# Zero-weight matmuls beside value matmuls, tile switches in the scheduler, and a lent score bank

## The chip, the cores and the metric

The kernel runs on one core of a Trainium2 chip. The metric is the device time of one execution in microseconds (us). The *granted clock* is the share of TensorE's full clock that the profile records as granted to it; 1 is full speed. Before the change it is 1780 us. All times below are medians; a run over 1.5% above the fastest of its kernel is called slow and left out of ratios.

## The reference

Four blocks in turn, each added to its input, on x of 2048 rows and 512 columns: A, B, A, B. Each has a layer norm ahead.

```python
# A: 32 heads of 16, one shared key and value head
q = (x @ wq).reshape(B, S, H, Dh).transpose(0, 2, 1, 3)
k, v = x @ wk, x @ wv
p = softmax(einsum("bhqd,bkd->bhqk", q, k) * Dh ** -0.5)
o = einsum("bhqk,bkd->bhqd", p, v)            # then heads side by side, @ wo
# B: linear attention, phi(t) = (t + 1 where t > 0, else exp(t)) + 1e-6
kv, z = einsum("bhsd,bhse->bhde", phi(k), v), phi(k).sum(s)
o = (phi(q) @ kv) / (phi(q) @ z + 1e-6)       # then @ wo
```

The weight of the work is A: 32 x 2048 x 2048 exponentials, twice. The kernel cuts them into 4096 *blocks* of 128 keys by 512 queries.

## The kernel before

The program holds its own list scheduler. It simulates the five engines with a duration for every operation, decides in what order each engine issues, and emits that fixed order with semaphores. What the simulation has wrong can therefore turn into waits on the chip: with the cost of a tile switch set to 0 in it, ScalarE waited 38.5 us for score matmuls instead of 4.2 (below).

Matmuls write into `ps`, which the program divides into eight *banks* of 512 columns, numbered 0 to 7. A block takes three steps: a score matmul (32 rows of the array, 128 columns), an exponential, and a value matmul (128 rows, 32 columns). ScalarE takes the exponentials of three blocks in one instruction. VectorE takes some blocks too, with a polynomial in six instructions.

```python
# scores: row group i, 32 rows                                            (L635)
x = e.matmul(bank(b0 + k), lhsT=Kr[r, m, kt*P:(kt+1)*P], rhs=QT[r, ...], start=True, stop=True)
# values: column group c, 32 columns, accumulated in bank 7               (L671)
e.matmul(ps[32*c:32*c+32, 7*512:8*512], lhsT=Vaug[:, kt, :], rhs=src, start=..., stop=...)
# ScalarE: three score banks at once (set 0: banks 0-2, set 1: banks 3-5) (L775)
e.activation(PTA[:, i, 0:m*512], bank(3*s, m*512), ACTF.Exp, scale=SCALE)
# VectorE: its scores are in bank 6                                       (L829)
e.tensor_scalar(out=xT[...], in0=bank(6), ...)
...
# set 1 filled with 2 blocks only, where bank 5 may be lent:
if s == 1 and SHARE and (not banks.free[5] or (not banks.free[6] and self.waiting())):
    w = 2
```

Bank 6 is shared: every projection, transpose and output tile needs it too. `SHARE` is False before, so bank 5 is never lent to them.

When the simulated TensorE has nothing to do and its recent activity is under a target, the scheduler adds a full-array matmul with zero weights into bank 7. It changes no result and is there to keep TensorE's clock up (with 461 of them instead of 1234 the clock was 0.937 to 0.951 instead of 0.997 to 1.000, below):

```python
FILL, FILLW, FILLN = 0.6, 1.7, 512
def streaming(now):          # activity over the last FILLW us
    ...
        st = {"pv": 0.071, "sA": 0.2, "dummy": 0.2}.get(o.name, 0.85 * o.dur[PE])
def idle(now):
    if not sc.order[PE] or streaming(now) > FILL * FILLW:
        return
    ...                                                                   # (L897)
    o = add(PE, 0.03 + FILLN*0.41e-3, lambda e: e.matmul(bank(7, FILLN), lhsT=zer[:],
            rhs=maskx[:].bitcast(BF16)[:, 0:FILLN], start=not owned, stop=True, ...), name="dummy")
```

The softmax here doesn't subtract the row's maximum and nothing guards it: scores larger than these inputs give would overflow.

## Time and profile before

| | before |
|---|---|
| time | 1780.14 us (1778.29 to 1781.13, 3 runs) |
| ScalarE / VectorE / TensorE busy | 97% / 87% / 95% |
| granted clock of TensorE | 0.998 |
| blocks on ScalarE / VectorE | 3618 / 478 |
| full zero matmuls | 1234 |

The first lines are from the page of the kernel before: busy us, share and instruction count of each engine, and the granted clock in tenths over 40 slices of the span.

```profile
PE 1683.0 (95%) x11642; PEld 533.4 (30%) x11642; DVE 1554.0 (87%) x2767; ACT 1728.1 (97%) x1452; POOL 31.3 (2%) x46
...
PEclk9999999999999999999999999999999999999999
```

The groups of the same page: line, engine, operation, output and inputs, shapes, count, then busy us and mean ns of one, then idle time of the engine before them and what ended it.

```profile
L775 ACT ACTIVATE PTA<-ps_all 128x1536 bf16<-128x1536 f32 x1207 | 1644.0, 1569 | 7.7 <-PE ps_all L635 6.3
L635 PE MATMUL ps_all<-QT,Kr 32*128 32x512 bf16 x4096 | 611.3, 385 | 39.8 <-ACT PTA L775 14.8
L671 PE MATMUL ps_all<-PTA,Vaug 128*32 128x512 bf16 x3618 | 520.1, 390 | 8.2 <-DVE Eo L683 7.8
L897 PE MATMUL ps_all<-maskx,zer 128*128 128x512 bf16 x1234 | 401.0, 386 | 0.0
L829 DVE TENSOR_SCALAR xT<-ps_all 128x512 int32<-128x512 f32 x478 | 327.4, 685 | 80.8 <-PE ps_all L635 78.9
```

ScalarE's exponentials take 1644 us and wait 7.7 us in all. Time can be won by giving ScalarE fewer blocks. VectorE could take more: it stands still 80.8 us ahead of L829, mostly for score matmuls.

Two stretches of 50 us of the kernel before, from the table of stretches: busy us and instructions of each engine, then the clock.

```profile
core 0: us, PE busy (x) PEld busy (x) DVE busy (x) ACT busy (x) POOL busy (x), PEclk, DMA share, GB/s
200.00:250.00 50.00, 47.55 (x324) 13.79 (x324) 47.52 (x83) 49.82 (x39) 0.99 (x1) 1.00 0.00 1
250.00:300.00 50.00, 47.39 (x340) 15.09 (x338) 36.23 (x61) 50.00 (x42) 0.00 (x0) 1.00 0.00 1
```

In the second stretch block B's projections for a part of the rows use bank 6, and VectorE falls from 47.5 to 36.2 us. That is what lending a second bank aims at.

Last, a piece of the timeline of the kernel before: start, duration, engine, line.

```profile
311.12 0.39 PE L635 MATMUL ps_all<-QT,Kr 32*128 32x512 bf16 x1
311.44 0.39 PE L671 MATMUL ps_all<-PTA,Vaug 128*32 128x512 bf16 x2
311.76 0.60 PE L897 MATMUL ps_all<-maskx,zer 128*128 128x512 bf16 x2
312.30 0.39 PE L635 MATMUL ps_all<-QT,Kr 32*128 32x512 bf16 x3
```

Two value matmuls in different column groups take as long as one (0.39 us for the two at 311.44, and 0.39 for a single one at 310.76). Two full matmuls take 0.60 where one takes 0.39, so a pass costs 0.21 us. From one tile shape to another the starts are 0.32 us apart: the change of shape costs about 0.11 us more than a pass.

### The profile page before, as it was taken

How to read it: one execution, taken by the hardware profiler on the slowest of the kernel's cores; microseconds unless marked ns; L12 is line 12 of the kernel's file. 1: busy time of each engine (PE TensorE's matmuls, PEld its weight loads, DVE VectorE, ACT ScalarE, POOL GpSimd, SP SyncE). 2: the span in 40 equal slices, each digit the busy share in tenths (PEclk: the TensorE clock that was granted, in tenths of full speed). 3: DMA queues.
4: the chain of work that ended last, by engine and by line, in shares of the span. 5: the costliest groups of instructions: out<-in, count | busy, mean ns of one | idle time of the engine just before them, and what ended most of it. 6: DMA issues, size and time to landing. Idle time of an engine off the chain costs nothing.

```text
span 1777.9 us, 27691 instructions
## 1 busy us (share of the span) xinstructions
PE 1683.0 (95%) x11642; PEld 533.4 (30%) x11642; DVE 1554.0 (87%) x2767; ACT 1728.1 (97%) x1452; POOL 31.3 (2%) x46
## 2 busy tenths in 40 slices
PE   7999999999999999999899999999999999999998
PEld 4222222222232222233442222322222322222334
DVE  7999997999887998878789999879998879978775
ACT  7999999999999999999699999999999999999996
POOL 0000000000000000000000000000000000000000
PEclk9999999999999999999999999999999999999999
DMA  3000000000000000000000000000000000000001
GB/s 120 1 1 1 1 1 1 1 1 1 1 1 1 1 1 1 1 1 1 1 1 1 1 1 1 1 1 1 1 1 1 1 1 1 1 1 1 1 1 48
DMA packets 7724, 9.14 MB, mean 5 GB/s; under 512 B 1456, under 2 KB 7088, under 8 KB 7600
## 3 DMA queue, kind: packets, MB, share of 16 engines
q1 hardware_dynamic: 7600, 7.37, 1.3%
q8 instruction: 91, 1.49, 0.3%
q14 instruction: 33, 0.27, 0.1%
HBM read 5.28 MB, written 2.10 MB: 4 GB/s over the span
## 4 chain that ended last, share of the span: by engine, by line
ACT 62%; PE 19%; DVE 17%; issue 1%; DMA 0%; POOL 0%; SPq 0%
ACT PTA L775 60%; PE ps_all L635 6%; PE ps_all L671 5%; PE ps_all L897 3%; DVE xT L829 3%; DVE PTD L851 3%; PE ps_all L496 2%; ACT e_buf L939 1%; DVE xs L847 1%; DVE xu L846 1%; DVE xs L850 1%; DVE stats L461 1%; PE ps_all L1060 1%; DVE xs L848 1%; DVE xu L849 1%
## 5 line engine op out<-in xcount | busy, mean ns | idle before, releaser
L775 ACT ACTIVATE PTA<-ps_all 128x1536 bf16<-128x1536 f32 x1207 | 1644.0, 1569 | 7.7 <-PE ps_all L635 6.3
L635 PE MATMUL ps_all<-QT,Kr 32*128 32x512 bf16 x4096 | 611.3, 385 | 39.8 <-ACT PTA L775 14.8
L671 PE MATMUL ps_all<-PTA,Vaug 128*32 128x512 bf16 x3618 | 520.1, 390 | 8.2 <-DVE Eo L683 7.8
L897 PE MATMUL ps_all<-maskx,zer 128*128 128x512 bf16 x1234 | 401.0, 386 | 0.0
L829 DVE TENSOR_SCALAR xT<-ps_all 128x512 int32<-128x512 f32 x478 | 327.4, 685 | 80.8 <-PE ps_all L635 78.9
L635 PEld LDWEIGHTS ps_all<-QT,Kr 32*128 32x128 bf16 x4096 | 147.2, 91 | 486.3 <-ACT PTA L775 188.1
L851 DVE SCALAR_TENSOR_TENSOR PTD<-xT,xs 128x1024 uint16<-128x1024 int32 x239 | 290.3, 1215 | 1.8
L671 PEld LDWEIGHTS ps_all<-PTA,Vaug 128*32 128x32 bf16 x3618 | 126.2, 93 | 319.0 <-issue 299.9
L846 DVE TENSOR_SCALAR xu<-xT 128x1024 f16<-128x1024 uint16 x239 | 164.3, 687 | 3.7
L847 DVE TENSOR_TENSOR xs<-xu 128x1024 f16<-128x1024 f16 x239 | 163.5, 684 | 2.9
L850 DVE TENSOR_TENSOR xs<-xs,xu 128x1024 f16<-128x1024 f16 x239 | 163.0, 682 | 2.4
L897 PEld LDWEIGHTS ps_all<-maskx,zer 128*128 128x128 bf16 x1234 | 93.9, 97 | 196.5 <-issue 179.4
L671 PE MATMUL ps_all<-PTD,Vaug 128*32 128x512 bf16 x478 | 128.8, 388 | 18.2 <-DVE Eo L683 11.4
L848 DVE TENSOR_SCALAR xs<-xs 128x1024 f16<-128x1024 f16 x239 | 98.9, 414 | 1.7
L849 DVE TENSOR_SCALAR xu<-xu 128x1024 f16<-128x1024 f16 x239 | 99.2, 415 | 0.0
L496 PE MATMUL ps_all<-wqkv_sb,xnT 128*128 128x512 bf16 x256 | 68.7, 382 | 1.5 <-DVE xT L829 0.9
L940 DVE TENSOR_SCALAR e_buf<-e_buf 128x512 f32<-128x512 f32 x64 | 27.1, 423 | 45.4 <-ACT e_buf L939 45.2
L469 POOL TENSOR_TENSOR rstd<-veps,mhalf 128x1 f32<-128x1 f32 x30 | 27.8, 925 | 1668.5 <-DVE veps L467 1668.5
L939 ACT ACTIVATE e_buf<-ps_all 128x512 f32<-128x512 f32 x64 | 46.0, 719 | 4.8 <-PE ps_all L496 3.1
L671 PEld LDWEIGHTS ps_all<-PTD,Vaug 128*32 128x32 bf16 x478 | 28.2, 93 | 65.2 <-DVE PTD L851 30.7
L461 DVE BATCH_NORM_STATS2 stats<-x_sb 128x6 f32<-128x512 bf16 x64 | 43.2, 680 | 3.8 <-DMA x_sb<-in_A_x_dram 2.9
L683 DVE COPY Eo<-ps_all 128x512 f32<-128x512 f32 x62 | 42.4, 684 | 4.3 <-PE ps_all L671 3.7
(87 smaller groups left out, 825.9 us busy)
## 6 DMA issues: line engine op xcount, KB each, us to landing
out_dram<-x_sb SPq DMA_DIRECT2D x16, 128.0 KB, 1.7
x_sb<-in_A_x_dram SPq DMA_DIRECT2D x3, 512.0 KB, 6.9
wqkv_sb<-in_B_wqkv_dram SPq DMA_DIRECT2D x1, 1536.0 KB, 11.3
x_sb<-in_A_x_dram SPq DMA_DIRECT2D x2, 256.0 KB, 3.1
wq_sb<-in_A_wq_dram SPq DMA_DIRECT2D x1, 512.0 KB, 5.1
wo_sb<-in_A_wo_dram SPq DMA_DIRECT2D x1, 512.0 KB, 8.3
wo_sb<-in_B_wo_dram SPq DMA_DIRECT2D x1, 512.0 KB, 10.9
wk_sb<-in_A_wk_dram SPq DMA_DIRECT2D x1, 16.0 KB, 2.5
```

Of the source, the lines that this page charges most:

```text
L496: i = e.matmul(bank(h.idx, n), lhsT=l, rhs=r, start=(c + k == 0), stop=(c + k == len(mms) - 1))
L635: x = e.matmul(bank(b0 + k), lhsT=Kr[r, m, kt * P:(kt + 1) * P], rhs=QT[r, self.units[u][0] % 2, gs, q0:q0 + n], start=True, stop=True)
L671: return e.matmul(ps[32 * c:32 * c + 32, 7 * 512:8 * 512], lhsT=Vaug[:, kt, :], rhs=src, start=opened[0], stop=opened[1], skip_group_check ...
L775: oe = add(AC, tac(m * 512), lambda e: e.activation(PTA[:, hp.idx, 0:m * 512], bank(3 * s, m * 512), ACTF.Exp, scale=SCALE), deps=[o] + pr ...
L829: o = add(DV, tdv(512), lambda e: e.tensor_scalar(out=xT[:, hx.idx, i * 512:(i + 1) * 512], in0=bank(6), scalar1=SCALE * LOG2E * 65536.0, ...
L846: o = add(DV, tdv(w, 0.52), lambda e: e.tensor_scalar(out=u_, in0=lo, scalar1=1.0 / 65536, scalar2=-0.5, op0=ALU.mult, op1=ALU.add), deps= ...
L847: o1 = add(DV, tdv(w, 0.52), lambda e: e.tensor_tensor(out=s_, in0=u_, in1=u_, op=ALU.mult), deps=[o] + c["prev"], name="xsq", **kw)
L848: o2 = add(DV, tdv(w, 0.26), lambda e: e.tensor_scalar(out=s_, in0=s_, scalar1=XK, scalar2=-XW, op0=ALU.mult, op1=ALU.add), deps=[o1], nam ...
L849: o3 = add(DV, tdv(w, 0.26), lambda e: e.tensor_scalar(out=u_, in0=u_, scalar1=1.0, scalar2=XL, op0=ALU.mult, op1=ALU.add), deps=[o1], nam ...
L850: o4 = add(DV, tdv(w, 0.52), lambda e: e.tensor_tensor(out=s_, in0=s_, in1=u_, op=ALU.mult), deps=[o2, o3], name="xc", **kw)
L851: o5 = add(DV, tdv(w), lambda e: e.scalar_tensor_tensor(out=PTD[:, hp.idx, 0:w].bitcast(U16), in0=xT[:, k, 0:w], scalar=2.0 ** -9, in1=s_, ...
L897: o = add(PE, 0.03 + FILLN * 0.41e-3, lambda e: e.matmul(bank(7, FILLN), lhsT=zer[:], rhs=maskx[:].bitcast(BF16)[:, 0:FILLN], start=not ow ...
```

## The change

Its intent has three parts. (1) *Riders*: zero-weight matmuls of 32 columns are started beside a value matmul, in column groups that it leaves unused, so that activity costs no time; full ones stay for when activity is low. (2) The scheduler models TensorE better: passes of 0.217 us, column groups side by side, and 0.1 us for a change of tile shape. (3) `SHARE = True`: bank 5 is lent. The diff, cut to its core (many changed durations left out):

```diff
+SWITCH, PASS = 0.1, 0.217
+    def pe_need(self, o):
+        k, g = o.pk
+        if k != self.pk:
+            return self.pend_t + SWITCH
+        return self.pend_t if k == "F" else max([self.pgrp.get(x, 0.0) for x in g])
...
-    FILL, FILLW, FILLN = 0.6, 1.7, 512
-    SHARE = False
+    AWIN, ATGT, AFREE = 2.4, 0.44, 0.6
+    SHARE = True
...
-    def streaming(now):
+    def activity(now):
...
+                k = o.pk[0]
+                w = RG / P * len(o.pk[1]) if k == "S" else 0.4 if k == "P" else 0.95
+                tot += w * (min(end, now) - max(o.t0, now - AWIN))
+        return tot / AWIN
...
+        if owned and last.pk[0] == "P" and now - last.t0 < 0.03 and a < AFREE:
+            for c in range(4):
+                if sc.pgrp.get(c, 0.0) <= now:
+                    o = add(PE, PASS, lambda e, c=c: e.matmul(ps[32*c:32*c+32, 7*512:8*512], lhsT=zer[:, 0:32],
+                                      rhs=maskx[:].bitcast(BF16)[:, 0:512], start=False, stop=True, ...), name="dp")
...
+        if a > ATGT:
             return
...     # then one full zero matmul, as before
```

`activity` counts a rider like a value matmul, at 0.4 of its time: both are of kind "P".

More of the change, by code (lines that the diff above doesn't have):

```diff
@@ L17 @@
 FLEX = 0.0
+SWITCH, PASS = 0.1, 0.217
 class Op:
     __slots__ = ("engs", "fn", "dur", "prio", "deps", "nleft", "succ", "rt", "guard", "acq", "uses", "rel", "cb",
-                 "eng", "t0", "vis", "idx", "gidx", "waits", "marked", "val", "vc", "dma", "done", "name")
+                 "eng", "t0", "vis", "idx", "pk", "gidx", "waits", "marked", "val", "vc", "dma", "done", "name")
 class Holder:
@@ L64, in __init__ @@
         self.idle = lambda now: None
+        self.pk, self.pgrp, self.pend_t = "F", {}, 0.0
     def add(self, engs, dur, fn, reads=(), writes=(), prio=5.0, guard=None, acq=(), uses=(), rel=(), cb=None, deps=(),
-            dma=False, name=""):
+            dma=False, name="", pk=("F", ())):
         o = Op()
+        o.pk = pk
         o.engs = engs if isinstance(engs, tuple) else (engs,)
@@ L128, in _try @@
             cand = sorted(ready, key=lambda r: (r[0] + (FLEX if len(r[2].engs) > 1 and self.act_ok(r[2]) else 0.0), r[1]))
+        limit = None
         for i, (p, s, o) in enumerate(cand):
@@ L131, in _try @@
                 continue
+            if e == PE:
+                need = self.pe_need(o)
+                if need > self.now + 1e-9:
+                    if limit is None or need < limit:
+                        limit = need
+                        self.at(need, None)
+                    continue
+                if limit is not None and self.now + o.dur[PE] > limit + 0.03:
+                    continue
             if e == AC and len(o.engs) > 1 and not self.act_ok(o):
@@ L167, in _start @@
         end = self.now + o.dur[e]
+        if e == PE:
+            if o.pk[0] != self.pk:
+                self.pk, self.pgrp = o.pk[0], {}
+            for x in o.pk[1]:
+                self.pgrp[x] = end
+            self.pend_t = max(self.pend_t, end)
         o.vis = end + (3.0 if o.dma else LAT[e])
-        self.tfree[e] = end
-        self.at(end, None)
+        self.tfree[e] = end if e != PE or o.pk[0] == "F" else self.now + 0.004
+        self.at(self.tfree[e], None)
         self.at(o.vis, None)
@@ L480, in tr @@
             return i
-        o = add(PE, 0.45, tr, reads=["ident"], deps=[o], uses=[hx], acq=[hb], rel=[hx], prio=prio, name="tr")
+        o = add(PE, 0.22, tr, reads=["ident"], deps=[o], uses=[hx], acq=[hb], rel=[hx], prio=prio, name="tr")
         def cp(e):
@@ L498, in proj @@
             kw = dict(acq=[h]) if c == 0 else dict(uses=[h], deps=[o])
-            o = add(PE, len(part) * (0.03 + n * 0.36e-3), f, reads=reads, prio=prio, name=name, **kw)
+            o = add(PE, len(part) * (0.006 + n * 0.42e-3), f, reads=reads, prio=prio, name=name, **kw)
         return o
@@ L527, in f @@
             return k
-        o = add(PE, 0.16 * n, f, reads=["wv"] + [("xnT", t) for t in range(t0, t0 + n)], acq=[h], prio=prio, name="vp")
+        o = add(PE, 0.1 * n, f, reads=["wv"] + [("xnT", t) for t in range(t0, t0 + n)], acq=[h], prio=prio, name="vp")
         def ev(e):
@@ L558, in q_tile @@
             kw = dict(acq=[h]) if c == 0 else dict(uses=[h], deps=[o])
-            o = add(PE, 0.55, f, reads=["wq", ("xnT", t)], prio=prio, name="qt", **kw)
+            o = add(PE, 0.445, f, reads=["wq", ("xnT", t)], prio=prio, name="qt", **kw)
         def ev(e):
@@ L667, in cb @@
                     self.norm(u, o)
+            c = (j % NRG) * (4 // NRG) + j // NRG
             def f(e):
-                c = (j % NRG) * (4 // NRG) + j // NRG
                 return e.matmul(ps[32 * c:32 * c + 32, 7 * 512:8 * 512], lhsT=Vaug[:, kt, :], rhs=src, start=opened[0], stop=opened[1],
                                 skip_group_check=True)
-            o = add(PE, 0.1, f, reads=[("V", kt)], deps=[dep], uses=[hold], rel=[hold] if last else [], prio=2.0 + 1e-4 * u, guard=guard, cb=cb, name="pv")
+            o = add(PE, PASS, f, pk=("P", (c,)), reads=[("V", kt)], deps=[dep], uses=[hold], rel=[hold] if last else [], prio=2.0 + 1e-4 * u, guard=guard, cb=cb, name="pv")
             return o
@@ L693, in tr @@
                 return i
-            o = add(PE, 1.0, tr, reads=["identf"], deps=[oe], acq=[ht, hos] if par == 0 else [ht], uses=[he], rel=[he], prio=1.2, name="trA")
+            o = add(PE, 0.48, tr, reads=["identf"], deps=[oe], acq=[ht, hos] if par == 0 else [ht], uses=[he], rel=[he], prio=1.2, name="trA")
             o = add(DV, 0.168, lambda e: e.reciprocal(rden[:, hr.idx, :].unsqueeze(2), bank(ht.idx).rearrange("p (a c) -> p a c", c=32)[:, :, DH:DH + 1]),
@@ L769, in f @@
                 return self.smm(e, got, 3 * s)
-            o = add(PE, 0.2 + 0.014 * m if RG == 32 else 0.05 + 0.14 * m, f, reads=self.keys(got), deps=prev, uses=[h], prio=0.0, name="sA")
+            o = add(PE, PASS * (-(-m * RG // P)), f, reads=self.keys(got), deps=prev, uses=[h], prio=0.0, name="sA",
+                    pk=("S", tuple(dict.fromkeys(self.parts(q)[0] for q in got))))
             hp = Holder(p_pta)
@@ L827, in dstep @@
             banks.hist[6] = []
-            o = add(PE, 0.22, lambda e: self.smm(e, [p], 6), reads=self.keys([p]), deps=prev, uses=[h], prio=1.5, name="sD")
+            o = add(PE, PASS, lambda e: self.smm(e, [p], 6), reads=self.keys([p]), deps=prev, uses=[h], prio=1.5, name="sD", pk=("S", (self.parts(p)[0],)))
             o = add(DV, tdv(512), lambda e: e.tensor_scalar(out=xT[:, hx.idx, i * 512:(i + 1) * 512], in0=bank(6), scalar1=SCALE * LOG2E * 65536.0,
@@ L874, in bass_interleave_layers__grouped_kv_mqa__linear_attn_block__prompt_kernel @@
     sc.step = ctl.step
-    def streaming(now):
+    def activity(now):
         tot = 0.0
         for o in reversed(sc.order[PE]):
-            if o.t0 + 1.5 < now - FILLW:
+            if o.t0 + 1.5 < now - AWIN:
                 break
-            st = {"pv": 0.071, "sA": 0.2 if RG == 32 else 0.4, "dummy": 0.2}.get(o.name, 0.85 * o.dur[PE])
             end = o.t0 + o.dur[PE]
-            if end > now - FILLW:
-                tot += st * min(1.0, (end - (now - FILLW)) / o.dur[PE])
-        return tot
+            if end > now - AWIN:
+                k = o.pk[0]
+                w = RG / P * len(o.pk[1]) if k == "S" else 0.4 if k == "P" else 0.95
+                tot += w * (min(end, now) - max(o.t0, now - AWIN))
+        return tot / AWIN
     def idle(now):
-        if not sc.order[PE] or streaming(now) > FILL * FILLW:
+        if not sc.order[PE] or any(not d.done or d.vis > now for d in (sc.lastw["mask"], sc.lastw["zer"])):
             return
@@ L892, in idle @@
         owned = u >= 0 and 0 < sum(ctl.count[u]) < 64
-        if not owned and not banks.free[7]:
+        if not owned and (not banks.free[7] or any(d.vis > now for d in banks.hist[7])):
             return
-        if owned and now < sc.tfree[AC] < now + 0.1:
-            return
-        o = add(PE, 0.03 + FILLN * 0.41e-3, lambda e: e.matmul(bank(7, FILLN), lhsT=zer[:], rhs=maskx[:].bitcast(BF16)[:, 0:FILLN], start=not owned, stop=True, skip_group_check=True),
+        last = sc.order[PE][-1]
+        a = activity(now)
+        if owned and last.pk[0] == "P" and now - last.t0 < 0.03 and a < AFREE:
+            for c in range(4):
+                if sc.pgrp.get(c, 0.0) <= now:
+                    o = add(PE, PASS, lambda e, c=c: e.matmul(ps[32 * c:32 * c + 32, 7 * 512:8 * 512], lhsT=zer[:, 0:32], rhs=maskx[:].bitcast(BF16)[:, 0:512],
+                                                              start=False, stop=True, skip_group_check=True),
+                            reads=["mask", "zer"], prio=9.0, pk=("P", (c,)), name="dp")
+                    banks.hist[7].append(o)
+                    sc._start(PE, o)
+                    return
+        if a > ATGT:
+            return
+        need = sc.pend_t + (0.0 if sc.pk == "F" else SWITCH)
+        if need > now + 1e-9:
+            sc.at(need, None)
+            return
+        if any(not o.done and not o.acq and (o.guard is None or o.guard()) for (_, _, o) in sc.ready[PE]):
+            return
+        if owned and now < sc.tfree[AC] + LAT[AC] < now + PASS + SWITCH:
+            return
+        o = add(PE, PASS, lambda e: e.matmul(bank(7), lhsT=zer[:], rhs=maskx[:].bitcast(BF16)[:, 0:512], start=not owned, stop=True, skip_group_check=True),
                 reads=["mask", "zer"], deps=[] if owned else list(banks.hist[7]), prio=9.0, name="dummy")
         banks.hist[7].append(o)
-        sc._try(PE)
+        sc._start(PE, o)
     sc.idle = idle
@@ L916, in tr @@
             return i
-        o = add(PE, 0.45, tr, reads=["ident", ("Osb", g % 2, 0), ("Osb", g % 2, 1)], acq=[h], uses=[hos], rel=[hos], writes=keys, prio=pr, name="otr")
+        o = add(PE, 0.22, tr, reads=["ident", ("Osb", g % 2, 0), ("Osb", g % 2, 1)], acq=[h], uses=[hos], rel=[hos], writes=keys, prio=pr, name="otr")
         def cp(e):
@@ L985, in pq_tile @@
             kw = dict(acq=[h]) if g == 0 else dict(uses=[h], deps=[o])
-            o = add(PE, 0.27, f, reads=["wqkv", ("xnT", t)], prio=pr, name="pq", **kw)
+            o = add(PE, 0.224, f, reads=["wqkv", ("xnT", t)], prio=pr, name="pq", **kw)
         phi(h, o, pqT[:, :, ts], [("pq", g, t) for g in range(NG)], 2.4, tiled=True)
@@ L1006, in kv_block @@
                 rd = [t] if i > 0 else tl
-                o = add(PE, 0.22, f, reads=[(k, tt) for k in ("pk", "vB") for tt in rd], prio=3.4, name="kv", **kw)
+                o = add(PE, 0.172, f, reads=[(k, tt) for k in ("pk", "vB") for tt in rd], prio=3.4, name="kv", **kw)
             dst = kvacc if b == 0 else kvtmp
@@ L1050, in den @@
             return i
-        o = add(PE, 0.3, den, reads=[("zb", g) for g in range(NG)] + [("pq", g, t) for g in range(NG)], acq=[win, hd], prio=pr - 0.4, name="den")
+        o = add(PE, 0.223, den, reads=[("zb", g) for g in range(NG)] + [("pq", g, t) for g in range(NG)], acq=[win, hd], prio=pr - 0.4, name="den")
         o = add(AC, tac(512), lambda e: e.activation(e_buf[:, he.idx, :], bank(hd.idx), ACTF.Ln, bias=1e-6), deps=[o], uses=[hd], acq=[he], rel=[hd], prio=0.4 + 0.01 * t, name="ln")
```

## The prediction

> **What bounds the kernel now.** By the page's busy table ScalarE works 1728.1 of 1777.9 us (97%), TensorE is marked 95%, VectorE 87%. The chain that ended last is 60% the ScalarE exponential (PTA, L775). In the table of stretches ScalarE is busy 1635 of 1643 us between 30:850 and 912:1735; nearly all its 50 us of idleness lie in the start, the layer change (850:912) and the tail. Steady time is won only by giving ScalarE less to do.
>
> The other exponential path is VectorE: 478 of 4096 score blocks. By the groups one block costs it 0.685 + half of (687+684+414+415+682+1215) ns = 2.73 us; one ScalarE block costs 1644/3618 = 0.454 us. VectorE is idle 189 us in the two steady stretches. The waits name the reason: L829 for score matmuls 78.9 us, e_buf for ScalarE 45.2, v_tok and x_sb for projections 36. L829 has one PSUM bank, shared with every projection, transpose and phi tile. In stretches without such work VectorE is busy about 49 of 50 us (20 blocks), with it 36 to 44 (10 to 12 blocks).
>
> **What the change does.**
> 1. SHARE lends bank 5 of the second ScalarE set to that other work; VectorE's scores keep bank 6. Cost: ScalarE fills of 2 blocks instead of 3. Chained 1536-column instructions take 1.343 us; at 0.83 ns a column about 0.064 us is fixed, so a two-block fill loses about 0.021 us. I estimate 200 to 450 such fills: 4 to 10 us.
> 2. Full-array zero matmuls (1234, 401 us marked) mostly give way to 32-column ones that start beside a value matmul. I estimate 1000 to 2500 riders and 200 to 600 full ones. [...]such tiles run concurrently; this trace agrees (three value matmuls in 0.40 us, one in 0.39), so riders should cost almost nothing.
> 3. The scheduler models the tile switch. [...]the trace shows weight-load gaps of 0.23 us ("issue") between score and value groups. This should cut badly placed waits of VectorE, not ScalarE's work.
>
> **Sum.** If half of VectorE's 189 us is recovered, that is about 34 more blocks: -34 x 0.454 = -15 us. Two-block fills: +6. Earlier score matmuls and projections at start and layer change: -5. Result: about 1763 us, -0.9%. All of VectorE's idleness would be worth 31 us before the fills' cost, so over 2% is unlikely.
>
> Predicted 1763 us, 8 in 10 between 1742 and 1784. Faster by over 2%: 0.13; within 2%: 0.80; slower by over 2%: 0.07.
>
> **What would show it.** Step 1: L829's count rises from 478 to about 512, its wait for score matmuls falls below 45 us, VectorE reaches 90 to 92%; L775 splits into 1536- and 1024-column forms. Step 2: far fewer 128-wide zero matmuls, many 32-wide ones, value-matmul groups as short as now. Step 3: ScalarE stays at 97%; its wait for score matmuls stays under 15 us. PEclk stays at 9.
>
> **What would make it wrong.** The target of TensorE's activity falls from 0.6 to 0.44, on another scale; if riders count for less than assumed, the granted clock (0.998 now) dips and both paths wait. If two-block fills are many hundreds, or the shorter instruction exposes the other set's refill, the gain is eaten. If start and layer change (each 10 to 15 us of ScalarE idleness) improve much, it could pass 2%.

"This trace agrees" in step 2 is the measurement that the forecast for riders rests on: three value matmuls take 0.40 us at 301.62 in before and one takes 0.39 at 300.65. The 0.83 ns a column of step 1 had no measurement beside it. The trace of after shows it: starts of chained exponentials are 1.331 us apart after three blocks and 0.905 after two, by the medians, so 0.426 us for 512 columns, with 0.05 us left as fixed where the prediction had 0.064.

## The result, and the profile after

| | before | after |
|---|---|---|
| time | 1780.64 us (4 runs) | 1873.89 us (1870.09 to 1882.06, 4 runs) |
| granted clock | 0.998 | 0.831 in the profiled run, 0.823 to 0.840 |
| ScalarE / VectorE busy | 97% / 87% | 93% / 87% |
| blocks on ScalarE / VectorE | 3618 / 478 | 3574 / 522 |
| full zero matmuls / riders | 1234 / 0 | 218 / 1376 |

The ratio is 1.0532, with a 95% interval of 1.0495 to 1.0569: 5.3% slower. Ratios here are the mean time of one kernel's fast runs over that of the other's of the same rounds, so not quite the ratio of the medians quoted. The counts of zero matmuls, blocks and two-block fills are read from the orders that the programs emit; the trace of after has its riders whole, but its group of full zero matmuls shows 128 of the 218.

The page of the kernel after, the same lines as before:

```profile
PE 1655.4 (88%) x11844; PEld 490.4 (26%) x12002; DVE 1636.2 (87%) x2944; ACT 1733.1 (93%) x1528; POOL 29.2 (2%) x46
...
PEclk9678878859896788988797787988769886888988
```

Its groups:

```profile
L803 ACT ACTIVATE PTA<-ps_all 128x1536 bf16<-128x1536 f32 (+1 forms) x1284 | 1646.8, 1430 | 91.0 <-PE ps_all L661 86.1
L661 PE MATMUL ps_all<-QT,Kr 32*128 32x512 bf16 x4096 | 738.0, 450 | 154.0 <-ACT PTA L803 111.6
L698 PE MATMUL ps_all<-PTA,Vaug 128*32 128x512 bf16 x3574 | 598.8, 457 | 5.3 <-DVE Eo L710 4.6
L929 PE MATMUL ps_all<-maskx,zer 128*32 128x512 bf16 x1376 | 439.8, 469 | 0.0
L857 DVE TENSOR_SCALAR xT<-ps_all 128x512 int32<-128x512 f32 x522 | 358.3, 686 | 93.2 <-PE ps_all L661 91.1
```

VectorE took more blocks, as meant. But the exponentials now wait 91 us, 86 of them for score matmuls, where they waited 7.7. A score matmul went from 385 to 450 ns on average, a value matmul from 390 to 457. Nothing was added to these matmuls; the clock under them went down (0.998 to 0.831). The table of stretches, cut along one stretch of low clock, the next of full clock and the next of low, shows the machine in both conditions:

```profile
core 0: us, PE busy (x) PEld busy (x) DVE busy (x) ACT busy (x) POOL busy (x), PEclk, DMA share, GB/s
52.60:86.30 33.70, 32.76 (x181) 6.96 (x182) 28.40 (x50) 28.39 (x21) 0.00 (x0) 0.50 0.00 0
86.90:120.40 33.50, 28.32 (x231) 8.71 (x230) 32.45 (x59) 33.43 (x29) 0.99 (x1) 1.00 0.00 1
120.90:144.30 23.40, 22.65 (x136) 4.89 (x136) 21.20 (x37) 21.05 (x16) 0.00 (x0) 0.50 0.00 1
```

At clock 1.00 ScalarE is busy 33.43 of 33.50 us. At 0.50 TensorE itself is full (32.76 of 33.70), ScalarE gets 28.39 and runs 21 instructions where it ran 29. There is no third value in this trace: its clock records have only 1.0 and 0.5. The low stretches last from 3.413 to 44.373 us, 635 us in 41 of them, and each is a whole multiple, 1 to 13 times, of the shortest. (A 42nd, of 0.39 us, lies at the end of the records, after the span.) The same records of before show two stretches of 3.413 us. In the longest low stretch of after TensorE was marked busy 42.75 of 44.30 us (376.50:420.80), and the clock stayed at half all the while.

The clock records and ScalarE's instructions together tell where ScalarE stood still. I added up, for each profiled run, the gaps between ScalarE's instructions that fall into low and into full clock (from the first clock record on, which comes 11.3 us after the start in before and 11.2 in after):

```
kernel                  low clock us   ScalarE idle in low clock   in full clock
before                          6.8                  1.6                38.4
after                         635                   99.3                31.0
```

The span grew by 1873.3 - 1777.9 = 95 us; ScalarE's idleness in the tally grew by 130.3 - 40.0 = 90 us and its work by 5. All of the growth falls into low clock (1.6 to 99.3 us); in full clock idleness did not grow (38.4 to 31.0 us, in a full-clock time that is some 530 us shorter, so this is no gain of the new order). So the loss lies in the low-clock stretches. What brought them about is a matter for experiments.

A piece of the timeline of after, in low clock:

```profile
68.33 0.61 PE L698 MATMUL ps_all<-PTA,Vaug 128*32 128x512 bf16 x3
68.33 0.61 PE L929 MATMUL ps_all<-maskx,zer 128*32 128x512 bf16 x1
68.73 0.63 PE L698 MATMUL ps_all<-PTD,Vaug 128*32 128x512 bf16 x1
68.73 0.63 PE L929 MATMUL ps_all<-maskx,zer 128*32 128x512 bf16 x1
```

Riders do run side by side with value matmuls and cost no pass of their own: three value matmuls and a rider, started together at 68.33, take 0.61 us. In full clock, at 101.72, they take 0.40 us, as three value matmuls without a rider do in before (at 301.62).

### The profile page after: what moved, and what is told of

It is laid out like the page before. It is cut to its first block, busy times and chain, and to the rows that moved or that the text cites. A ratio compares the mean times of both kernels' runs of the same rounds, so it can differ in the third digit from the quotient of the medians.

```text
span 1873.3 us, 28558 instructions
## 1 busy us (share of the span) xinstructions
PE 1655.4 (88%) x11844; PEld 490.4 (26%) x12002; DVE 1636.2 (87%) x2944; ACT 1733.1 (93%) x1528; POOL 29.2 (2%) x46
## 4 chain that ended last, share of the span: by engine, by line
ACT 53%; PE 34%; DVE 12%; issue 1%; DMA 0%; SPq 0%; POOL 0%; ACTq 0%
ACT PTA L803 50%; PE ps_all L661 14%; PE ps_all L698 12%; DVE xT L857 2%; PE ps_all L719 2%; PE ps_all L522 2%; DVE PTD L879 2%; ACT e_buf L987 1%; PE ps_all L945 1%; PE ps_all L1108 1%; DVE xs L875 1%; DVE xs L878 1%; DVE xu L874 1%; DVE stats L487 1%; PE ps_all L929 1%
## 5 line engine op out<-in xcount | busy, mean ns | idle before, releaser
L803 ACT ACTIVATE PTA<-ps_all 128x1536 bf16<-128x1536 f32 (+1 forms) x1284 | 1646.8, 1430 | 91.0 <-PE ps_all L661 86.1
L661 PE MATMUL ps_all<-QT,Kr 32*128 32x512 bf16 x4096 | 738.0, 450 | 154.0 <-ACT PTA L803 111.6
L698 PE MATMUL ps_all<-PTA,Vaug 128*32 128x512 bf16 x3574 | 598.8, 457 | 5.3 <-DVE Eo L710 4.6
L929 PE MATMUL ps_all<-maskx,zer 128*32 128x512 bf16 x1376 | 439.8, 469 | 0.0
L857 DVE TENSOR_SCALAR xT<-ps_all 128x512 int32<-128x512 f32 x522 | 358.3, 686 | 93.2 <-PE ps_all L661 91.1
L879 DVE SCALAR_TENSOR_TENSOR PTD<-xT,xs 128x1024 uint16<-128x1024 int32 x261 | 316.8, 1216 | 0.8
L698 PE MATMUL ps_all<-PTD,Vaug 128*32 128x512 bf16 x522 | 169.0, 470 | 13.7 <-DVE PTD L879 10.9
L929 PEld LDWEIGHTS ps_all<-maskx,zer 128*32 128x32 bf16 x1376 | 89.8, 97 | 1.1 <-issue 0.8
L719 PE MATMUL ps_all<-identf,Eo 128*128 128x128 f32 x256 | 58.3, 369 | 3.9 <-DVE Eo L710 1.7
L945 PE MATMUL ps_all<-maskx,zer 128*128 128x512 bf16 x128 | 54.9, 472 | 1.6 <-issue 0.9
```

The costliest lines, as they stand in the source:

```text
L661: x = e.matmul(bank(b0 + k), lhsT=Kr[r, m, kt * P:(kt + 1) * P], rhs=QT[r, self.units[u][0] % 2, gs, q0:q0 + n], start=True, stop=True)
L698: return e.matmul(ps[32 * c:32 * c + 32, 7 * 512:8 * 512], lhsT=Vaug[:, kt, :], rhs=src, start=opened[0], stop=opened[1], skip_group_check ...
L803: oe = add(AC, tac(m * 512), lambda e: e.activation(PTA[:, hp.idx, 0:m * 512], bank(3 * s, m * 512), ACTF.Exp, scale=SCALE), deps=[o] + pr ...
L857: o = add(DV, tdv(512), lambda e: e.tensor_scalar(out=xT[:, hx.idx, i * 512:(i + 1) * 512], in0=bank(6), scalar1=SCALE * LOG2E * 65536.0, ...
L879: o5 = add(DV, tdv(w), lambda e: e.scalar_tensor_tensor(out=PTD[:, hp.idx, 0:w].bitcast(U16), in0=xT[:, k, 0:w], scalar=2.0 ** -9, in1=s_, ...
L929: o = add(PE, PASS, lambda e, c=c: e.matmul(ps[32 * c:32 * c + 32, 7 * 512:8 * 512], lhsT=zer[:, 0:32], rhs=maskx[:].bitcast(BF16)[:, 0:51 ...
```

## The experiments

The theory: the clock falls because 1016 full zero matmuls were taken out and what replaced them, the riders, does not hold it up. Rivals: riders do as much as the scheduler assumes and only the target is too low; the lent bank or the new order exposes ScalarE, and the clock is a symptom; it is their zero data that makes riders worthless. Fifteen kernels were run, each beside the kernel before on the same chip. "Fills of two" are ScalarE instructions of two blocks.

### The bank lent alone

```diff
 # before.py
-    SHARE = False
+    SHARE = True
```

> The kernel before with the bank lent (SHARE = True) and nothing else of the change; its schedule has 1070 full zero matmuls, 542 VectorE score blocks and 362 two-block ScalarE fills. My theory (the loss comes only from the granted clock, the lent bank is sound): clock stays above 0.98, ScalarE's wait for score matmuls below 20 us, time 1780 - 64 x 0.454 + 362 x 0.021 = about 1759 us (1750 to 1772). Rival (the lent bank and the short fills themselves expose ScalarE and VectorE to waits): 1785 us or more at a clock above 0.98.

Measured: 1801.30 us, ratio 1.0118 (1.0092 to 1.0144), clock 0.992 to 0.999. Here my theory was wrong and the rival right: in the old order lending loses 1.2% at a high clock. The wait of ScalarE for score matmuls in this kernel (us in total, times, longest):

```profile
ACT PTA L775 <- PE ps_all L635: 32.2, 91, 1.0
```

Before, this wait was 6.3 us in 23 waits. By my tally ScalarE is idle 67.1 us in full clock. In a list of its gaps of over 0.1 us in full clock ahead of L775 (29.9 us in all), 22.5 us stand right behind an instruction of two blocks: it ends about 0.4 us sooner than one of three, and the other set is not refilled yet. (Starts of chained exponentials are 1.331 us apart after three blocks and 0.904 after two, by the medians; that is 0.83 ns a column and 0.05 us fixed, so by itself a two-block fill loses about 0.02 us, as the prediction said.) A two-block fill thus costs more than its own overhead (22.5 us of gaps behind 362 of them are 0.06 us each), unless the order knows better.

### The riders not emitted, all else in the same order

```diff
 # after.py
+    gone = {id(o) for o in sc.all if o.name == "dp"}
+    sc.all = [o for o in sc.all if id(o) not in gone]
+    sc.order[PE] = [o for o in sc.order[PE] if id(o) not in gone]
...  # renumber, and take them out of the dependencies
     sc.finalize()
```

> The kernel after with exactly its order on every engine, but the 1376 riders are not emitted. My theory (a rider beside a value matmul adds no activity[...]): clock as after, 0.83 within 0.02, time 1874 us within 12. Rival (riders count as the scheduler assumes, 0.4 of their time, and only the target is too low): the activity falls by a further 0.07 of each stretch, so clock below 0.75 and time above 1920 us.

Measured: 1882.21 us, ratio 1.0565 (1.0521 to 1.0609), clock 0.813 to 0.833. Its clock row:

```profile
PEclk9778879668997569988797787879679875798888
```

Taking away 1376 riders moved the clock by some 0.01 to 0.02 and the time by less than the intervals tell apart (after: 1.0495 to 1.0569). The rival's clock below 0.75 did not come. These 1376 riders hold the clock up little or not at all.

### Both targets raised

```diff
 # after.py
-    AWIN, ATGT, AFREE = 2.4, 0.44, 0.6
+    AWIN, ATGT, AFREE = 2.4, 0.6, 0.75
```

> The kernel after with both activity targets raised (0.44 to 0.60, riders 0.60 to 0.75): 696 full zero matmuls, 1779 riders, 518 VectorE blocks, 271 two-block fills. My theory (too few full zero matmuls let the clock fall to half in stretches, and this is the whole loss): clock above 0.95, ScalarE's wait for score matmuls below 25 us, time 1755 to 1785 us. Rival (new order, tile-switch model and lent bank lose the time, the clock is a symptom of the waits): clock may rise but the time stays above 1820 us.

Measured: 1766.53 us (1761.55 to 1777.56), ratio 0.9940 (0.9904 to 0.9976), clock 0.979 to 0.995. With 696 full zero matmuls instead of 218 the loss is gone and a gain of 0.6% stands. Its clock row and ScalarE's wait for score matmuls:

```profile
PEclk9999999999999999999999999999999999999999
...
ACT PTA L803 <- PE ps_all L661: 4.2, 9, 0.6
```

The lent bank, the new scheduler and the riders are all still there, so none of them was the loss. Its four runs also show the price of the clock: 1761.55 us at 0.995, 1764.32 at 0.993, 1768.75 at 0.987, 1777.56 at 0.979.

### Full zero matmuls only

```diff
 # after.py
-    AWIN, ATGT, AFREE = 2.4, 0.44, 0.6
+    AWIN, ATGT, AFREE = 2.4, 0.56, -1
```

> The kernel after without any rider and the full target at 0.56: 926 full zero matmuls, 515 VectorE blocks, 294 two-block fills. My theory: clock above 0.98, time 1780 - 37 x 0.454 + 294 x 0.021 = about 1769 us (1758 to 1778), so faster than before, without a single rider. Rival (riders are needed to hold the clock once the full ones are cut by a quarter): clock below 0.95, time above 1790 us.

Measured: 1772.12 us, ratio 0.9970 (0.9949 to 0.9992), clock 0.983 to 0.991. As expected: no rider is needed.

### The zero matmuls of before made narrow

```diff
 # before.py, L897
-    e.matmul(bank(7, FILLN), lhsT=zer[:], rhs=...
+    e.matmul(ps[0:32, 7 * 512:7 * 512 + FILLN], lhsT=zer[:, 0:32], rhs=...
```

> The kernel before with its 1234 full zero matmuls made 32 columns wide (128 rows, alone in the array, same places in the order). My theory ([...]a rider fails because a value matmul streams at the same time anyway): clock above 0.98, time 1780 to 1800 us. Rival A (a 32-column zero matmul is seen as a quarter of the array, or not at all, wherever it stands): clock below 0.90, time above 1830 us.

Measured: 1772.51 us, ratio 0.9968 (0.9948 to 0.9989), clock 0.989 to 0.998. From its page:

```profile
PEclk9999999999999999999999999999999999999999
...
L897 PE MATMUL ps_all<-maskx,zer 128*32 128x512 bf16 x1234 | 398.2, 384 | 0.0
```

The very instruction that is worthless as a rider, 32 columns with zero weights, holds the clock nearly as well as a full one when it streams alone (0.989 to 0.998, against 0.997 to 1.000 of before in the same round). So neither its width nor its zeros can be what fails it in the change; what is left of the differences is that another matmul of the same shape streams at the same time. "Nearly" has to be said: low clock takes 37.5 us of its trace, against 6.8 before. The time came out below the expected 1780. A narrow zero matmul has the tile shape of the value matmuls, and the idle time of weight loads ahead of L897 falls from 196.5 to 74.1 us; that this is what saved the time is not shown, for ScalarE's wait for score matmuls did not fall (8.9 us, 6.3 before).

### The target of before lowered

```diff
 # before.py
-    FILL, FILLW, FILLN = 0.6, 1.7, 512
+    FILL, FILLW, FILLN = 0.42, 1.7, 512
```

> The kernel before with its target lowered (0.60 to 0.42): 461 full zero matmuls instead of 1234, 484 VectorE blocks; no lent bank, no riders, no tile-switch model. My theory: the cut of full zero matmuls alone brings the clock down, to 0.80 to 0.95, time 1800 to 1870 us. Rival (the clock falls only with the new order or the lent bank): clock above 0.985, time below 1785 us.

Measured: 1811.46 us, ratio 1.0201 (1.0151 to 1.0250), clock 0.937 to 0.951. From its page:

```profile
PEclk9999989957899989999999989997999999899999
```

With 461 full zero matmuls and nothing else of the change, the old order loses its clock as well.

### Riders with non-zero weights

```diff
 # after.py, L929
-    lhsT=zer[:, 0:32], rhs=...
+    lhsT=ident[:, 0:32], rhs=...
```

> The kernel after with riders that hold the identity in place of zeros, so that they carry non-zero weights (the result is wrong on purpose). My theory (concurrency, not zero data, makes a rider worthless): clock as after, 0.83 within 0.03, time 1860 to 1890 us. Rival B[...]: clock above 0.90, time below 1830 us.

Measured: 1875.96 us, ratio 1.0545 (1.0524 to 1.0566), clock 0.829 and 0.831. No change. Rival B, that zero weights are the cause, had expected a clock above 0.90, so they are not. This test is weaker than the one with narrow zero matmuls, because the identity has one non-zero weight in a column and the moving operand is mostly zero. (The small error it adds stayed within the tolerance of the comparison.)

### The new scheduler alone

```diff
 # after.py
-    AWIN, ATGT, AFREE = 2.4, 0.44, 0.6
-    SHARE = True
+    AWIN, ATGT, AFREE = 2.4, 0.55, -1
+    SHARE = False
```

> The kernel after without riders and without the lent bank, target 0.55: 967 full zero matmuls, 461 VectorE blocks, practically no two-block fills; so the tile-switch model alone, at a high clock. My theory (the model alone wins nothing, because ScalarE was not waiting before; it only makes lending safe): clock above 0.98, time 1780 + 17 x 0.454 = about 1788 us (1780 to 1796). Rival (the model by itself is the gain seen in the kernels with target raised): below 1773 us.

Measured: 1784.57 us, ratio 1.0034 (1.0019 to 1.0049), clock 0.989 to 0.991. As the theory had it: without a lent bank the model of the tile switch wins nothing.

### A corrected count of activity

```diff
 # after.py, in activity(); and AWIN, ATGT, AFREE = 1.7, 0.48, -1
-                w = RG / P * len(o.pk[1]) if k == "S" else 0.4 if k == "P" else 0.95
-                tot += w * (min(end, now) - max(o.t0, now - AWIN))
+                lo, hi = max(o.t0, now - AWIN), min(end, now)
+                if k == "P":                      # value matmuls side by side count once
+                    tot += max(0.0, min(hi, seen) - lo)
+                    seen = min(seen, lo)
+                else:
+                    tot += (RG / P * len(o.pk[1]) if k == "S" else 0.95) * (hi - lo)
```

> The kernel after without riders and with its activity count corrected[...]: time in which value matmuls of any column group stream counts once, score matmuls by a quarter each, full ones in full; window 1.7 us, target 0.48. 728 full zero matmuls, 520 VectorE blocks, 339 two-block fills. My theory (the count, not the amount, was wrong): clock above 0.98 with fewer full zero matmuls than the 926 of the kernel with full ones only, time 1755 to 1770 us. Rival (any saving of full zero matmuls below about 900 costs clock without riders): clock below 0.97, time above 1778 us.

Measured: 1795.78 us, ratio 1.0087 (1.0057 to 1.0117), clock 0.961 to 0.976. A miss. Counting in this way did not let the amount fall: 728 full zero matmuls placed this way hold the clock less well than the 696 of the kernel with both targets raised (0.979 to 0.995). Target and window were changed along with the count, so this run doesn't say which of them is short; that stays open.

### The same with narrow zero matmuls

```diff
 # on top of the corrected count
-    e.matmul(bank(7), lhsT=zer[:], rhs=...                      # kind "F"
+    e.matmul(ps[0:32, 7 * 512:8 * 512], lhsT=zer[:, 0:32], rhs=...  # kind "P", no switch beside values
```

> The same with its zero matmuls 32 columns wide and alone in the array (701 of them), so that they need no tile switch beside value matmuls; 518 VectorE blocks, 338 two-block fills. My theory: clock above 0.98, ScalarE's wait for score matmuls below 8 us, time 1750 to 1768 us, no slower than with full ones. Rival (narrow ones hold the clock less well here): clock more than 0.02 below the kernel with full ones, time above 1775 us.

Measured: 1804.52 us over six runs, clock 0.945 to 0.971; two runs were slow, and the four fast ones give 1.0075 (1.0029 to 1.0121). Also a miss, and no gain of narrowness shows through: the four fast runs have a median of 1795.7 us and clocks of 0.950 to 0.971, its sister 1795.8 us and 0.961 to 0.976, too close to call.

### Targets raised, riders not emitted

The edit of the riders not emitted, on the kernel with both targets raised.

> The kernel with both targets raised, exactly its order, with its 1779 riders not emitted. My theory (a rider neither holds the clock nor costs time): clock within 0.015 of the 0.98 to 0.995 that the kernel with riders shows, time 1760 to 1778 us. Rival (at a high clock the riders do hold the clock up): clock below 0.95, time above 1790 us.

Measured: 1774.82 us over six runs, ratio of its fast runs 0.9946 (0.9925 to 0.9967). The four fast runs had clocks of 0.980 to 0.990, two slow ones 0.947 and 0.959 (1808.84 and 1796.86 us). The fast runs fit the theory; the slow ones left a doubt, taken up below.

### The bank lent in the old order, with narrow zero matmuls

The edits of the bank lent alone and of the narrow zero matmuls together.

> The kernel before with the bank lent and its zero matmuls 32 columns wide (1070 of them): same order as the kernel with the bank lent alone (1801 us, ScalarE waits 32 us for score matmuls). My theory (lending lost in the old order because tile switches that its scheduler does not know delay score fills, and a full zero matmul between value and score matmuls makes one switch more): ScalarE's wait for score matmuls below 20 us, time 1778 to 1793 us. Rival (the lent bank's short fills themselves are late, whatever the zero matmuls): wait and time unchanged, 30 us or more and 1795 to 1806 us.

Measured: 1791.24 us, ratio 1.0051 (1.0018 to 1.0085), clock 0.978 to 0.996, ScalarE's wait 26.3 us. Between the two: some 10 us better than 1801 us, which fits that unneeded tile switches are a part of what lending cost there, and not the whole. Again the narrow ones hold the clock a little less well in the same order: 47.8 us of low clock against 23.9.

### The tile switch taken out of the model

```diff
 # after.py, targets raised to 0.6 and 0.75
-SWITCH, PASS = 0.1, 0.217
+SWITCH, PASS = 0.0, 0.217
```

> The kernel with both targets raised (0.60, 0.75), its scheduler told that a tile switch costs nothing (SWITCH 0.1 to 0.0); the durations stay the new ones. 908 full zero matmuls, 1638 riders, 542 VectorE blocks, 262 two-block fills. My theory (knowing the switch is what keeps ScalarE's refills in time under the lent bank): clock above 0.98, ScalarE's wait for score matmuls 20 us or more, time 1772 to 1800 us, although 24 more blocks on VectorE would by themselves save 11 us. Rival (the switch term is not needed; the new durations do it): wait below 10 us, time 1745 to 1760 us.

Measured: 1807.43 us, ratio 1.0155 (1.0137 to 1.0172), clock 0.986 to 0.991; the loss is larger than the expected 1772 to 1800. ScalarE's wait for score matmuls:

```profile
ACT PTA L803 <- PE ps_all L661: 38.5, 79, 2.3
```

One number in the scheduler, 0.1 us, is worth 41 us at nearly the same clock: 4.2 us of wait with it, 38.5 without. By my tally ScalarE's idleness in full clock is 72.7 us without it and 32.7 with it. In these orders it is what makes lending safe. The order that follows differs in more than its waits: 542 blocks on VectorE instead of 518, and 908 full zero matmuls instead of 696. The zero matmuls are not the reason: the next kernel has 909, knows the switch, and takes 1775.14 us. Whether the 24 more blocks have a share in the loss was not tested.

### A higher target, with and without riders

```diff
 # after.py; the second kernel has the same order with the riders not emitted
-    AWIN, ATGT, AFREE = 2.4, 0.44, 0.6
+    AWIN, ATGT, AFREE = 2.4, 0.66, 0.75
```

> The kernel after with targets 0.66 and 0.75: 909 full zero matmuls, 1752 riders, 517 VectorE blocks, 307 two-block fills. My theory: clock above 0.985 in every run, time 1758 to 1770 us, less scatter than at 0.60 (1762 to 1778). Rival (more full zero matmuls crowd TensorE and ScalarE waits): clock above 0.985 but wait for score matmuls above 20 us and time above 1775 us.

> Exactly the order of the kernel with targets 0.66 and 0.75, its 1752 riders not emitted. Theory (riders add nothing): median clock within 0.005 of the kernel with riders, time within 5 us. Rival (riders add a little, as the slow runs of the other pair hint): median clock lower by 0.008 to 0.03, time longer by 6 to 25 us.

Measured with riders: 1775.14 us, ratio 0.9971 (0.9954 to 0.9988), clock 0.989 to 0.996 in six fast runs. Without: 1776.87 us, ratio 0.9970 (0.9952 to 0.9989), clock 0.988 to 0.995 in five fast runs, and one slow run at 0.973. The fast runs are the same with 1752 riders and without. In the two pairs of one order, three of the 12 runs without riders were slow and none of the 10 with them; whether riders help a little against it, the runs do not settle. The time itself missed the expected 1758 to 1770 us: with 909 full zero matmuls instead of 696 the clock is no higher (0.979 to 0.995 there). ScalarE's wait for score matmuls in its profiled run:

```profile
ACT PTA L803 <- PE ps_all L661: 19.1, 18, 5.3
```

That was 4.2 us with 696. It does not show that more zero matmuls crowd TensorE: of ScalarE's gaps of over 0.1 us ahead of the exponentials, 11.7 us lie in that run's low clock and 7.7 in full clock, against 1.1 and 3.6, so most of the rise goes with its 37.5 us of low clock.

### All kernels by the tally

The profiled runs, from the clock records and ScalarE's gaps as above:

```
kernel                       low clock us   ScalarE idle in low   in full clock
old order  before                    6.8              1.6              38.4
           bank lent                23.9              5.9              67.1
           bank lent, narrow        47.8             10.6              54.5
           narrow zeros             37.5              5.8              36.1
           target lowered          194.6             34.3              33.2
new order  after                   635               99.3              31.0
           riders not emitted      697              104.8              30.4
           targets raised           17.1              6.8              32.7
           full only                34.1             10.2              34.8
           corrected count         102.4             28.3              38.9
           switch not modelled      30.7              7.6              72.7
           riders non-zero          643               99.7              31.6
           scheduler alone          37.5              9.1              36.6
           corrected, narrow       170.7             35.8              36.7
           raised, no riders        71.7             17.2              34.1
           higher                   37.5             11.8              39.8
           higher, no riders        41.0             12.6              39.2
```

Two effects stand apart. In each us of low clock ScalarE stood still 0.15 to 0.4 us. In full clock, ScalarE stands still 29 us longer where the bank is lent without the tile switch in the model (old order), 40 us in the new order and 16 with narrow zero matmuls.

## Why the prediction was wrong

*The step that failed.* The prediction said "PEclk stays at 9" and forecast that the full zero matmuls "mostly give way to 32-column ones", as if these did the same work. It weighed what a rider costs, and that was right. It did not weigh what a rider is worth, though keeping the clock up is the only purpose of a zero matmul. In their place the runs showed: the clock fell to 0.831 with riders and to 0.815 without them, and ScalarE stood still 99.3 us in the stretches of low clock; the clock returned to 0.979 to 0.995 with 696 full zero matmuls. The text named this danger ("if riders count for less than assumed, the granted clock dips") and gave a loss of over 2% 7 in 100. The numbers for a warning were there: 1234 full zero matmuls of 0.21 us are 259 us of streaming, 15% of the span, in a kernel that already showed two short stretches of low clock. A kernel that dipped even with all of them could not lose four fifths on trust.

*What bounds the kernel* was right: ScalarE, for as long as the clock holds. In the after kernel it holds two thirds of the time (635 of 1873 us are low).

*Lending and VectorE's blocks* were sized well: 522 blocks against about 512, and 276 two-block fills in the trace against 200 to 450. VectorE's share, which was to reach 90 to 92%, stayed at 87% in after and is 92% with the targets raised. VectorE's wait for score matmuls was to fall below 45 us; it rose to 91.1 in after, and falls to 24.2 with the targets raised. But the reading that the tile-switch model touches only VectorE's waits was wrong in kind. It "should cut badly placed waits of VectorE, not ScalarE's work"; in fact it guards ScalarE against its own shorter instructions: ScalarE's wait for score matmuls is 4.2 us with it and 38.5 with the switch set to 0. Without it lending loses (1.0118 in the old order, 1.0155 in the new).

*The counts of step 2* were right: 1376 riders, 218 full ones.

*The sum.* With the clock restored, the kernel with targets raised takes 1766.5 us, where the sum had said 1763. That the total comes so close is in part luck. In its profiled run the exponentials take 1628.2 us instead of 1644.0, so 15.8 less where the terms for blocks and fills gave 9, and ScalarE is idle 3.6 us less in the start and the layer change (0:30 and 850:912), where the sum had 5. So the sum had the right terms and about the right size for a kernel whose clock holds, and the missing term is the clock: about 99 us of ScalarE's idleness in 635 us of half clock.

*How far the cause is settled.* Shown: the loss lies in low-clock stretches; raising only the two targets removes it; removing only the riders changes next to nothing; a narrow zero matmul alone does hold the clock (0.989 to 0.998). Not settled: how much each kind of matmul does for the clock, and by what rule it falls. The corrected count was an estimate, and no run confirmed it: built on it, the kernel was expected above 0.98 and showed 0.961 to 0.976. Nor did any run part the score matmuls' share from that of the others.

*A version that beats both.* The kernel with both targets raised: 1766.5 us, 0.6% under before and 5.7% under after by the medians.

## What to carry to other kernels

A filler that costs nothing may also do nothing: before trading it for another, measure on the chip what it is there for, here the granted clock, with the filler taken out and all else in the same order (here 0.823 to 0.840 with 1376 riders and 0.813 to 0.833 without). When a span gets longer with the same instructions, look at the clock row first, and then split the idle time of the bound engine by clock. And where a scheduler fixes the order, check that it knows the cost of a tile switch before giving the bound engine shorter instructions: here they paid only when it did (ratio 0.9940 with the switch at 0.1 us; 1.0155 with it at 0, and 1.0118 in the old order without it).
